# A gated recurrence and a long convolution on one core: batch 0's inputs ahead of the filter, and a filter that is rotated by its loads

## The chip, the cores and the metric

The kernel runs on one core of a Trainium2 chip. The metric is the device time of one execution in microseconds (us), lower is better. The kernel before was run three times: 457.23, 458.74 and 460.05 us, median 458.74. One further execution was recorded by the hardware profiler; all durations below are from it.

## The reference

Inputs are x and f_logit (4 x 6272 x 256), a lower bound per channel, a projection (256 x 768), a filter (6272 x 256) and an output projection (256 x 256), all float32.

```python
sig = 1 / (1 + exp(-f_logit))
f = lower_bound + (1 - lower_bound) * sig
h = f[:, t] * h + (1 - f[:, t]) * x[:, t]      # for t in range(S): a scan over time, per batch and channel
proj = h_all @ w_proj                          # x1, x2, x3: 256 columns each
x2_conv = irfft(rfft(x2, n=S) * rfft(filter, n=S), n=S)   # circular, along time, S = 6272 = 49 * 128
out = (x1 * x2_conv * x3) @ w_out
```

## The kernel before, in words

Time is split as 6272 = 49 x 128, and the Fourier transform is done in two factors by matmuls: one of length 128 (contracted over partitions) and one of length 49 (98 with real and imaginary parts).

For each batch b the work is:

- **hgrn(b)**, L317 to L382: 13 chunks of 512 time steps (the last has 128). Two loads of 512 KB on SyncE's queue (L332), the sigmoid on ScalarE (`sig`, L335), the product with x on GpSimd (`u`, L337), then per half of the channels (`kh`) sixteen transposes on TensorE (`su`, L349), the affine step that makes f (`f`, L362 on ScalarE or L364 on VectorE) and the scan on VectorE (`scan`, L370), which writes h into HA in f16. The start of h is copied behind its end (`wrap`, L378) for the circular shifts.
- **spectrum(b)**, L842: `P` (L714) makes x2 in 13 groups of up to four residues, evacuated by `x2`; it needs all 26 scans of the batch. `F1` (L727) is the transform of length 128, `F2` (L790) of length 49, `prod` the product with the filter's spectrum (on VectorE straight from PSUM, L813, or a copy and a GpSimd product, L822), `I2` (L832) the first inverse factor with its evacuation `Th` (L837).
- **gate(b)**, L385: `x13` (L398) projects x1 and x3, `xs` evacuates x1 and x3 or multiplies them on VectorE (L419), `z` (L428) multiplies on GpSimd. The result lies in `zt`.
- **phase_o(b)**, L882: the second inverse factor `I1` (L895), the gate `y` on VectorE (L901), the output projection `proj` (L913), its evacuation `o` and the store.

Before batch 0 the filter's spectrum is made once, in `prepare` (L436): 13 loads of 512 KB (`ff`, L619: four contiguous rows per partition), a cast to fp32r into `afs` (`fr`, L624), 49 matmuls with a rotated identity `rot` (L630), which put each residue's samples on the right partitions, and two evacuations per group (`f2`, L634) into the two tiles `f2` with gaps between the columns. Then 16 units of `FF1` (L655, two halves each), `afs` (L660), `FF2` (L673) and `hw` (L678), and stores of the spectrum to DRAM (`hst`, L682), from where each unit of each batch loads it again (`H`, L768).

TensorE also has 24 groups `warm` (L600) of four matmuls on the identity, which nothing reads.

The order is written out by hand of a planner: `ORDER` (L124) is a table of words, each an operation's number, the engine that does it and its PSUM bank (`order`, L98). `emit` (L107) issues the operations in the table's sequence, so each engine's queue is in that sequence; the `r` and `w` lists of `op` become semaphore waits by way of the tiles. VectorE's word `MUL` means the direct product (L813, L419). The cost figures in the calls of `op` were the planner's; they issue nothing.

Read out of the table, the order of the kernel before is: the filter's 13 loads first, then the loads of batch 0; on TensorE the 49 rotations with ten `warm` groups among them, then the 16 units of `FF1` and `FF2` interleaved with the transposes of batch 0, then `last`, then `P` of batch 0 (first with `x13` of chunk 0 just before it), then F1, F2, I2 mixed with `x13` of chunks 1 to 12 and the first transposes of batch 1. The other 14 `warm` groups stand later: three in the middle, eleven at the end.

Of the kernel before, what the change touches and what calls it, by code (L numbers as in the profile page):

```python
# [35 lines left out]
WARM = 24  # L36
# [12 lines left out]
AW = 4096  # L49

# [6 lines left out]
def m0_of(r):  # L57
    return (128 * q_of(r) - r) // Q


class Plan:
# [75 lines left out]
    "J0EJ1YGoIGpSJ4FJ3UGqCJ5sJ6YJ7VGvgGwWJ9FGtQGuIGyGG5SG4gHVUHWEJ8WKAQKCAKBRG0uGzYGxYG1YKDBJ+uJ/YG6YG9qG+YHCUG7qHEEH"
    "LWKEYG2QHBgHGsHFYHNGG3AKFTKHDKGWKIuKKUG8YHDYKMEHTQHKgG/SHMYHOYHUAHPuHQYHHYHXUHACKLWHYEKNuKOYHIQHeSHdgHZUHJAHaEHR"
    "WHiqHjYHgqHnQHSGHbUHcMHfYHoYHrAHmgHsYHpoHqYKPTKRDIBWICGHvgHwRKQTHyJKSrH4gHhYHkUHzYHxYH0pH1YHlEIDWILgIEGH5QHtUH7o"
    "H8YH6YHuEIHSIICIFWIGGH9oH+YKTYKUUKWMKVVKZQKXFKYYH2SH3CKbIIUgIJWIMUIKOIOsINYIQEIRYMkQMlAIdgIVSImgIZCMmIH/WIXqIAGI"  # L140
    "YYIWYIPYMoUMpEMqMNEgKaTKcDIvQIwAIaYISWIfYI5gKJYIeSMwQIgKIhYITGIiqIjYIbUMxAMyIKeSIcEKdYNFgKgCM0WM1GInUIzSIrsIsYIp"
    "EIqYNQgIoYJCgI0CIkQIlAM2OKfUKjVKkSKlFKhsNGANHYI6QKmqKnYI8oI+oI/YI9YNRgIxWIyGI1UItSI2EM8WJLgMngIuCI3UI4MI7YJDQJFo"
    "M9GNASJGYNcgJEYJHAJIYM+ONBCJAUKoRKpQNSANTYKqBNCKNIWJBENJGKroKsYKtRKvBJNYNMUJMSNNENKOJOCNOMJUgKuQKyRKzWJPYKwoKxYN"
    "dgJQqNeANogK3XK4SK0BK1GNpgK2YK5HK6qJVUJRYK7YNfYJXENUQNVAK8WNWIK+GNYTNygNzgMrgNZDK9SK/CLAYLBXLCWJJQNaLLGSJZsLDHLE"
    "uLFYNqALIKJKAJaYJSTJTDLHXNgQNkVN8gNhANlFLJvLKYNbgNiILLUNrYLMSLQTLNEJYYLRXLOqNmNLSDLVUKiYLTHN9gLXEM/gJWYNsQNtALWS"
    "NvTLYqLZYN0ANwDLUYLaVLPYNuINxLJbWJcGOHgN1YLbSR8QR9RLfWLcFNnYLdqLeYLgOR+AR/BN+ALkULlMN2SN/YOGgN3CN4KN5QNXYOQgN6AN"
    "7ILhWLiGLmUNDALuSLvKNPYLpWLnELqOOIAOAQOBAOCILjgORgODUObgOagOJYLwSOEELxCLrWLsGLtgOFML4QL5ILogOKSOSANLgLzWONUOlgOk"
    "gL0OOOEOLCL6QL7AL1WL9QL8gL2GOcAMzAOPMOTYOMKL+IMCUOUWOXSOYCMDMVAgOZKU/gL/QOVGOWOMAAOdYMEUMFEMHSMIKOeQOfAOgIOhUVLg"
    "OiEM3YVMgOjMOmASBWSCXSEHSDGMJSMKCOnYOoQOpIOrWOsGOqIMBgNjAOtOVXgLygMMUMRSVYgVNAMNMMSKL3gVBAO2QPAWO8UO3IMLgO9EPBGM"
    "GgPCSPDKPEQPFIO0UO1EVZAO4SO+WOwQO5KO/OVCYOySOzCVaYOuUOvEO6WO7GMOSPGUPHEOxIMPCMWQMXIPMUMQgPKWPLOPNEMTSMUCPIQPOUMY"  # L150
    "WPPEPJIMbQMcISAYPQSPRKPbYMZGPSUPWsPUsP8gPVYPaQPeoPXYSFYPTYPyWPcAPdYPzGMVgSGSSICSHQSLTSJoPqWSNDPiUPmEPuGPYSPZCSMR"
    "SQVSRQQFgPksPnYSOpQOgPlYSSFSToPfYPgSPhCPjYPvYP0UP1ESVXSXHPsuPtYQXgP2QP3IPoSPpCP9UQBsPrYP4WSUYP5GVOYSWQSaRScBP/sQ"
    "qgQAYPwSP6WP7OQHYP+YQCYPxCSbRSdBSYoQGUQIEQJYSeYQKsQzgVDSVECQgQQhAVFKQLYQDWQQYQEGQPUQRsQYQQaAQTsQUYQ8gQkSQlCQMWQc"
    "oQbYRFgQdYQZYSfQQNGSgUQiSQSYShAQjCSkVQmWMagQnGSmNQVQQWAQrSSisSjYVHUVjgQtqQoWQpOQvCQwYSZYVkgSlQSnoSpRQeSVIEVJMQuY"
    "SrBQfCQsYQ0WQ4GQ2uQ3YQ5YRYgVPQVQAVTSVwgVvgRhgQxUVRIVUCVVKQ1YSqXSuWQyESsHStYRQUQ+YSwGRSQRREQ9WQ/uRBuRGSRTARKCQ6UR"
    "HYROQRCYQ7ERIqSoYVGYRPARLYRJYSvWSzTS1DSxuRAYRqgRDUS0XS2vVlAVmYS3YMdQMeAMfgRZSRbqRdqRcYRUWVbQREES4SSPYSyYVKgRVGRW"
    "URXMRaYVcAVxAVdIRMWRjYRNGS5TS7DVfUV7gV8gRrWVnQS6CVyYS8YReYRvGVWYRzgVgMVoAVhMVpIVrSWHgWIgRtGS9XS+UVegVqgS/HTAsVsC"
    "VtKRfVRsYRgFRwYTCXTDQTHRTIWTEHTFoTGYTJBTKuRiURuYRksV9AVzSV0CRmEV3QWSgWRgV1KTMWTLYTOGRnYV+YTNXTPvTRUTTETSVTUtTWWV"
    "4AV5IRxSTQYTXXTbURyCTcVTgSTYGThTTdETZvWJAWKYTetTiKRlYRoQR1YTjrTkYRpAR0UR4ER2sV/WR3YWDQWbgWcgTBYWAGWBOWEATlSTmTTn"
    "CTorTpYTfYR5YTqUTsETrVTttTvSTwUWLWTuYTxCWFITyETzYR6SWMGWNOR7CT0UT1VT2ET3tTVYTaYT5QT6RT7AT8pT9YT+SabQSKYWTAT4YT/K"  # L160
# [34 lines left out]
def kernel(  # L195
# [801 lines left out]
```

## Time and profile before

| what | value |
|---|---|
| median of three runs | 458.74 us |
| span of the profiled execution | 455.6 us |
| TensorE (PE) busy | 439.6 us, 6009 matmuls |
| VectorE (DVE) busy | 407.4 us |
| ScalarE (ACT) busy | 402.3 us |
| GpSimd (POOL) busy | 308.8 us |
| DMA | 120.74 MB, 265 GB/s mean |

The runs shown are of other executions than the profiled one, so the span is not one of the three; it is 3.1 us below their median.

A row of the groups reads: line, engine, operation, output from inputs with their shapes and types, count, then the total busy time and the mean of one in ns, then the idle time before them with what ended it. A row of the stretches reads: start:end, length, busy us of PE, PEld (weight loads), DVE, ACT and POOL with the number of instructions of each, TensorE's granted clock, the DMA share and GB/s. A row of the time line reads: start, length, engine, line, operation. TensorE's matmuls overlap, so the sum over groups is above the busy time of the engine.

### The profile page before, as it was taken

Reading aid. Unit: us, or ns where it says so; the run is one execution under the profiler, and the core shown is the slowest. Engines: PE = TensorE matmul, PEld = TensorE weight load, DVE = VectorE, ACT = ScalarE, POOL = GpSimd, SP = SyncE. Lnnn points to the kernel's source line nnn. Section 1 sums busy time; section 2 is a strip of 40 time slices with the busy share of each in tenths; the row PEclk is TensorE's granted clock in tenths of the full one; section 3 lists DMA queues with packets and bytes.
Section 4 is the critical chain, followed back from the end, with each engine's and each line's share of the span. In section 5 each row is a group of like instructions: output and inputs, shape, how many; then the busy total and the mean of one; then the engine's idle time right before and its main releaser. Section 6 shows DMA issues by size and latency. Waiting matters only on the chain.

```text
span 455.6 us, 14635 instructions
## 1 busy us (share of the span) xinstructions
PE 439.6 (96%) x6009; PEld 348.4 (76%) x6009; DVE 407.4 (89%) x476; ACT 402.3 (88%) x577; POOL 308.8 (68%) x279
## 2 busy tenths in 40 slices
PE   7899999999999999999999999999999999999998
PEld 5687778677767888777668888777778896776797
DVE  8899997799999996999999977999999976989873
ACT  5899999899999987899989998999989858987563
POOL 8888973878899542788995626899994405696400
PEclk9599999999999999999999999999999999999999
DMA  8999999767898985479776896778759721765186
GB/s 326 387 371 345 378 375 361 279 187 233 299 300 282 340 300 237 169 232 374 253 264 219 285 315 272 237 250 303 261 177 317 301 95 46 248 187 185 47 321 246
DMA packets 44434, 120.74 MB, mean 265 GB/s; under 512 B 4304, under 2 KB 7632, under 8 KB 44368
## 3 DMA queue, kind: packets, MB, share of 16 engines
q1 hardware_dynamic: 44368, 119.82, 74.5%
q8 instruction: 47, 0.77, 0.7%
q14 instruction: 19, 0.16, 0.1%
HBM read 86.12 MB, written 31.98 MB: 259 GB/s over the span
## 4 chain that ended last, share of the span: by engine, by line
PE 72%; DVE 11%; ACT 9%; issue 4%; DMA 3%; POOL 1%; SPq 0%; ACTq 0%; DVEq 0%; POOLq 0%
PE PS L398 17%; PE PS L714 9%; PE PS L832 9%; PE PS L913 8%; PE PS L790 7%; DVE HA L370 7%; PE PS L727 6%; PE PS L349 6%; PE PS L895 4%; ACT fTs L362 2%; DMA X<-in_moe_filter_fft_dram 2%; PE PS L600 2%; ACT HA L284 2%; DVE ys L901 1%; ACT X L284 1%
## 5 line engine op out<-in xcount | busy, mean ns | idle before, releaser
L337 POOL TENSOR_TENSOR XT<-XT,FL 128x1024 f32<-128x1024 f32 (+1 forms) x49 | 109.9, 2247 | 55.7 <-ACT FL L335 38.5
L370 DVE TENSOR_TENSOR_SCAN HA<-fTs,HA,PS 128x512 f16<-128x512 f32 (+1 forms) x96 | 112.7, 1202 | 2.0 <-ACT fTs L362 1.1
L398 PE MATMUL PS<-HA,W 128*128 128x490 f16 (+1 forms) x416 | 100.2, 367 | 0.3 <-ACT Th L284 0.2
L822 POOL TENSOR_TENSOR PP<-HA,Hu 98x1008 f16<-98x1008 f16 x42 | 88.0, 2106 | 5.6 <-ACT HA L284 2.6
L284 ACT CAST HA<-PS 128x1024 f16<-128x1024 f32 (+1 forms) x101 | 81.2, 831 | 3.3 <-POOL PP L822 0.8
L901 DVE TENSOR_TENSOR ys<-PS,zt 128x1024 fp32r<-128x1024 f32 (+1 forms) x52 | 58.3, 1151 | 14.0 <-PE PS L895 10.3
L813 DVE TENSOR_TENSOR PP<-PS,Hu 98x1008 f16<-98x1008 f32 x54 | 63.6, 1199 | 1.5 <-PE PS L790 0.7
L362 ACT ACTIVATE fTs<-PS,nomc 128x512 f32<-128x512 f32 (+1 forms) x90 | 59.5, 680 | 4.5 <-PE PS L349 4.2
L398 PEld LDWEIGHTS <-W 128*128 128x128 f16 x416 | 35.3, 97 | 30.2 <-issue 2.9
L428 POOL TENSOR_TENSOR zt<-XS 128x490 f16<-128x490 f32 (+1 forms) x26 | 31.8, 1223 | 39.0 <-DVE ys L901 27.4
L913 PE MATMUL PS<-Wo,ys 128*128 128x256 f32 x392 | 57.5, 293 | 0.4 <-DVE ys L901 0.3
L286 ACT ACTIVATE XS<-PS 128x490 f32<-128x490 f32 (+1 forms) x88 | 51.0, 590 | 6.8 <-DVE zt L419 2.6
L832 PEld LDWEIGHTS <-PP 98*128 98x128 f16 x1024 | 49.2, 98 | 10.1 <-POOL PP L795 1.3
L284 ACT CAST Th<-PS 128x784 f16<-128x784 f32 x63 | 52.0, 828 | 3.4 <-PE PS L832 2.7
L913 PEld LDWEIGHTS PS<-Wo,ys 128*128 128x128 f32 x392 | 49.6, 188 | 4.5 <-DVE ys L901 1.2
L832 PE MATMUL PS<-VA,PP 98*128 98x98 f16 x512 | 52.1, 207 | 0.2 <-POOL PP L795 0.2
L832 PE MATMUL PS<-VB,PP 98*128 98x98 f16 x512 | 51.8, 207 | 0.0
L419 DVE TENSOR_TENSOR zt<-PS,XS 128x490 f16<-128x490 f32 (+1 forms) x78 | 49.2, 648 | 2.7 <-ACT XS L286 0.8
L335 ACT ACTIVATE FL<-FL 128x1024 f32<-128x1024 f32 (+1 forms) x49 | 49.8, 1022 | 0.6 <-DMA FL<-in_f_logit_dram 0.6
L714 PE MATMUL PS<-W,HA 128*128 128x256 f16 x392 | 44.6, 273 | 1.1 <-ACT X L284 1.1
L714 PEld LDWEIGHTS <-HA 128*128 128x128 f16 x392 | 42.9, 142 | 2.0 <-issue 1.3
L349 PE MATMUL PS<-iden,FL 64*128 64x64 f32 x736 | 41.7, 229 | 2.6 <-ACT PP L286 0.6
(119 smaller groups left out, 778.7 us busy)
## 6 DMA issues: line engine op xcount, KB each, us to landing
FL<-in_f_logit_dram SPq DMA_DIRECT2D x45, 512.0 KB, 5.3
XT<-in_x_dram SPq DMA_DIRECT2D x45, 512.0 KB, 6.2
Hu<-H SPq DMA_DIRECT2D x39, 512.0 KB, 4.6
out_dram<-osb SPq DMA_DIRECT2D x24, 512.0 KB, 4.6
out_dram<-PP SPq DMA_DIRECT2D x16, 512.0 KB, 4.8
Hl<-H SPq DMA_DIRECT2D x13, 512.0 KB, 4.7
X<-in_moe_filter_fft_dram SPq DMA_DIRECT2D x9, 512.0 KB, 7.0
out_dram<-HA SPq DMA_DIRECT2D x8, 512.0 KB, 5.7
```

The lines of the kernel that those rows point to most:

```text
L284: nc.scalar.copy(dst, src)
L337: op("u", {"POOL": 0.1 + 0.553 * nb}, lambda e, xt=xt, ft=ft: nc.gpsimd.tensor_tensor(xt, xt, ft, op=AOP.mult), r=[("ft", k)], w=[("xt", k)])
L349: nc.tensor.transpose(bank(pb)[:, at[p] + j:at[p] + hn:nb], src[ps, j, cols], iden[ps, ps])
L362: nc.scalar.activation(fT, sT, AF.Identity, scale=by, bias=1.0)
L370: nc.vector.tensor_tensor_scan(h, fT, bank(pb)[:, 512 - hn:512 + hn], init, op0=AOP.mult, op1=AOP.add),
L398: nc.tensor.matmul(PS[:, p, 0:n], W13[:, kh, js], HA[:, HB[kh] + t0:HB[kh] + t0 + n], start=(kh == 0), stop=(kh == 1))
L714: nc.tensor.matmul(pp[:, r - r0, :], column(HB[kh], q_of(r)), W2[:, kh, :], start=(kh == 0), stop=(kh == 1))
L813: nc.vector.tensor_tensor(pr, px.unsqueeze(1).broadcast_to([TB, 2, UE, 63]), hh(), op=AOP.mult)
L822: nc.gpsimd.tensor_tensor(pr, spec[:, o, :, 1:64].unsqueeze(1).broadcast_to([TB, 2, UE, 63]), hh(), op=AOP.mult)
L832: nc.tensor.matmul(PS[:, ib + o, pr * TB:(pr + 1) * TB], PP[:TB, k, o, n, 2 * pr:2 * pr + 2, :], v[:TB], start=(n == 0), stop=(n == 1))
L901: nc.vector.tensor_tensor(late["ys"][:, yk, :, 0:rn * 128], PS[:, cb:cb + 2, 0:rn * 128], late["zt"][:].rearrange("p k r m -> p k (r m)") ...
L913: nc.tensor.matmul(po[:, i, :], late["ys"][:, yk, kh, i * 128:(i + 1) * 128], Wo[:, kh, :], start=(kh == 0), stop=(kh == 1))
```

## The change

Batch 0 is computed ahead of the filter. Its chunks use six slots instead of four: three in `XF` (x and f together) and three lent by the X2 tile. The filter is loaded behind them. The rotation by matmul is gone: the loads fetch the rows already rotated, as `raw[m] = filter[49 m + 128 q mod 6272]`, group by group of q, each in up to three pieces (below the wrap, above it, and sixteen or more partitions across it from `EF`, a copy in DRAM of the filter's end and start, which two DMAs DRAM to DRAM write). A run of four rows of one partition, 4 KB contiguous before, is four runs of 1 KB now. Each group is then copied straight from the slot into the tiles `f2h` and `f2t` by three copies (`fr`), so one of the two copies per element goes, and the 49 matmuls with it. With `rot` go its two casts on VectorE.

The tiles are placed anew: `zt` is there from the start, so that gate(0) needs no `cz`; `PP`, `Hu`, `zp` and one `osb` are made when `FF1` of units 0 to 6 is done (`turn0`), where `f2h` was. `afs` has three half buffers instead of four halves, so `FF2` is eight matmuls of 256 columns instead of four of 512. `hw` uses the slots of chunk XF[0] for units 0 to 7 (each of its two halves twice), then `Hu` and `osb`. `warm` is eight groups at the start and six among the first transposes. `P` takes its columns in the order of q, and `phase_o` reads them back through `q_of`. `u` may be done on VectorE.

The table is new. Read out of it:

- SyncE: loads of chunks 0 to 4, then 6, 5, 7, 8, 9, 10, with the two `EF` copies between them; the filter's groups 0 to 5 among the loads of chunks 11 and 12; groups 6 and 7 into XF[0], so after the transposes of chunk 12; then 10, 9, 12, 11. 35 loads of filter pieces instead of 13 loads; 22 wraps on this queue instead of 13.
- VectorE: the table arguments (`args0`, `args1`), then for batch 0 24 scans of 512 and two of 128, 17 direct products and 4 evacuations of x1, 3 small table writes and one `f` of 128; then 4 `x2`, 7 `fr` and two gate operations; then, beside `FF1` and `FF2`, 17 `afs`, 5 `hw` and six others; then, up to the first `P` of batch 1, 24 scans of 512 and two of 128, 21 direct products with the spectrum, 11 `y`, 4 `zm` and seven others.
- TensorE: eight `warm`, the 26 transposes (`su`) of batch 0 with 45 `x13` (up to chunk 11) and six `warm` among them, the 13 groups of `P`, then the 16 units of `FF1` and `FF2` with four `F1` and two `x13` among them, `last`, and from there the units of batch 0 with the first seven chunks of batch 1.
- `FF1` of unit 0 needs the first `fr` of all 13 groups.

```diff
-WARM = 24
+WARM = 8
+E0, E1 = 5184, 6272
+NH2 = 56
+def wrap_of(q):
+    return -((128 * q - S) // Q)
...
+    XS = konst.tile([128, 4, XR * Q], F32, name="XS")
+    zt = konst.tile([128, 2, Q, 128], F16, name="zt")
+    EF = dram.tile([2 * (E1 - E0), D], F32, name="EF")
+    lent = X2[:, 0:NX * 4096].bitcast(F32).rearrange("p (k a j d) -> p k a j d", a=2, j=4, d=D)
...
-                k = c % (NX + len(more))
+                k = c % (2 * NX)
...
+                if b == 0 and c < 6 and kh == 0:
+                    op("warm", {"PE": 0.435}, warm, r=["iden"], w=["qT"], take=1)
...
+        slots = [(XF[:, k, a], [(t, k)]) for k in range(NX) for a, t in enumerate(("xt", "ft"))]
+        raws = slots[2:6] + rings + slots[0:2]
+        turns = (0, 1, 2, 3, 4, 5, 6, 7, 0, 1, 2, 3, 6)
+        hws = [(lambda i=i: XF[:, 0, i].rearrange("m r d -> m (r d)").bitcast(F16).rearrange("m (a n) -> m a n", a=2),
+                [("xt", 0), ("ft", 0)][i:i + 1]) for i in range(2)] * 2
...
+        afs = tmp.tile([128, 3, 2, UE // 2, 64], F32R, name="afs")
+        def rows_at(t, n0, m0, m1, q0, rn):
+            o = t[0:1, :]
+            return bass.AP(tensor=o.tensor, offset=o.offset + (n0 + Q * m0 + 128 * q0) * D,
+                           ap=[[Q * D, m1 - m0], [128 * D, rn], [1, D]])
+        for i in range(2):
+            op("ef", {"SP": 0.46}, lambda e, i=i: nc.sync.dma_start(
+                EF[i * (E1 - E0):(i + 1) * (E1 - E0), :].rearrange("(p r) d -> p (r d)", p=64),
+                ff[E0 * (1 - i):E0 * (1 - i) + E1 - E0, :].rearrange("(p r) d -> p (r d)", p=64)),
...
-               lambda e, raw=raw, fr=fr, rn=rn: copy(e, fr[:, 0:rn], raw[:, 0:rn]),
...
-                    nc.tensor.matmul(pr[:, r - r0, :], rot[:, m0_of(r):m0_of(r) + 128],
-                                     fr[:, r - r0, :], start=True, stop=True)
-            for p in range(2):
-                op("f2", either(128 * rn), lambda e, pb, r0=r0, rn=rn, p=p: copy(
-                    e, both(fv[p][:, :, r0:r0 + rn]),
...
+            for i, src, p0, p1, n0 in parts:
+                   nc.sync.dma_start(raw[p0:p1, 0:rn], rows_at(src, n0, p0, p1, q0, rn)),
...
+            for h, (p, j0, nj) in enumerate(((0, 0, NH2), (1, NH2, 64 - NH2), (1, 64, 64))):
+                    copy(e, both(fv[p][:, at:at + nj, q0:q0 + rn]), src[:, j0 // 64, j0 % 64:j0 % 64 + nj])
...
+                for h in range(2):
+                    for r in range(2):
+                        for e2 in range(2):
+                            nc.tensor.matmul(PS[:, pb + e2, 256 * h:256 * h + 256], FTr[rows, r, 0:M],
+                                             afs[rows, at[h], r], start=(r == 0), stop=(r == 1))
...
-                        nc.tensor.matmul(pp[:, r - r0, :], column(HB[kh], q_of(r)), W2[:, kh, :],
+                        nc.tensor.matmul(pp[:, r - r0, :], column(HB[kh], r), W2[:, kh, :],
...
-                        c0 = (rr * Q + r) * 128
+                        c0 = (rr * Q + q_of(r)) * 128
...
+        D1r, FTr = prepare(tmp)
+        hgrn(0)
+        free_x2()
+        last = filters(head, tmp, D1r, FTr)
```

More of the change, by code (lines that the diff above doesn't have):

```diff
@@ L639, in prepare @@
[L639 to L646 removed]
+            op("warm", {"PE": 0.435}, warm, r=["iden"], w=["qT"], take=1)
@@ L840, in unit, with spectrum @@
            r=["cv"], w=[("Th", u)], src=i2)
-    def spectrum(b):
+    def spectrum(b, last=None, turn=None):
         phase_p(b)
@@ L847, in spectrum @@
                 phase_f1(b, u)
+            if last and q == 0:
+                small_spectrum(last, turn)
             mini(b, q)
```

389 lines of the change are left out of this document (192 added, 197 removed).

## The prediction

> **What bounds the kernel now.** I read the page first (busy shares, slices), then the busy time by stretches, then the time line at the borders of the stretches.
>
> ```profile
> PE 439.6 (96%) x6009; PEld 348.4 (76%) x6009; DVE 407.4 (89%) x476; ACT 402.3 (88%) x577; POOL 308.8 (68%) x279
> ```
>
> TensorE (PE) is busy for 96%, so it looks like the bound. But three engines lie close together, and the stretches show that they take turns:
>
> ```profile
> core 0: us, PE busy (x) PEld busy (x) DVE busy (x) ACT busy (x) POOL busy (x), PEclk, DMA share, GB/s
> 0.00:23.00 23.00, 18.40 (x90) 14.37 (x91) 19.13 (x49) 15.76 (x25) 19.75 (x40) 0.78 0.93 358
> 23.00:71.50 48.50, 45.74 (x598) 36.34 (x599) 46.99 (x53) 48.29 (x74) 40.64 (x44) 1.00 1.00 367
> 71.50:97.00 25.50, 24.96 (x262) 20.16 (x261) 19.85 (x22) 22.96 (x31) 17.32 (x14) 1.00 0.78 270
> 97.00:143.10 46.10, 45.49 (x696) 32.12 (x693) 44.82 (x52) 45.03 (x69) 40.17 (x32) 1.00 0.84 272
> 143.10:167.10 24.00, 23.35 (x422) 20.48 (x421) 23.83 (x25) 23.10 (x34) 13.37 (x10) 1.00 0.88 308
> 167.10:455.60 288.50, 281.65 (x3952) 224.90 (x3950) 252.76 (x281) 247.17 (x348) 177.52 (x142) 1.00 0.67 235
> ```
>
> Up to 23 us only the filter is rotated. From 23 to 71.5 ScalarE (48.29 of 48.5) and VectorE (46.99) are the bound: the scans of batch 0 run beside the filter's FF1 and FF2. At 71.5 FF2 is done and P of batch 0 starts; from 97 on all three engines are full, VectorE with 68.65 of 70.1 us (98%). At 167.1 P of batch 1 starts, and it can't start before batch 1's last scan:
>
> ```profile
> 163.65 2.37 DVE HA L370 x2
> 166.06 1.08 PE PS L895 x32
> 167.14 10.65 PE PS L714 x96
> ```
>
> So the border to watch is P of batch 1. What TensorE has left from there is the same in both tables but for three groups of warm, so I carry the 288.5 us over and work out when the border falls.
>
> **The change, part by part.** What goes on TensorE:
>
> ```profile
> L630 PE MATMUL PS<-afs,rot 128*128 128x256 f32 x49 | 11.7, 388 | 2.5 <-POOL afs L296 2.4
> L600 PE MATMUL PS<-iden 128*128 128x256 f16 x96 | 14.0, 307 | 1.4 <-POOL iden masks.py:199 1.4
> 447.45 1.48 PE L600 MATMUL PS<-iden 128*128 128x256 f16 x12
> ```
>
> The rotations (11.7 us) and ten warm groups lie before 23 us, where TensorE has nothing else: alone they bring nothing. Three warm groups in the middle (twelve matmuls, 1.48 us by the last row) lie where it is full: -1.5 us. Eleven stand at the end behind or between the last waits: 0. What the new order can win is the useful work in the first 23 us; what it can lose is overlap. I add it up along the engine that ends each stretch last.
>
> *1. Start of the scans.* They queue on VectorE behind the table arguments, whose last operations are these, first with GpSimd busy beside them, then with it mostly idle, and GpSimd's u:
>
> ```profile
> 4.68 1.27 DVE L517 TENSOR_SCALAR PP<-HA 128x520 f32<-128x520 f32 x1
> 5.99 1.28 DVE L518 TENSOR_SCALAR PP<-PP 128x520 f32<-128x520 f32 x1
> 7.31 1.44 DVE L519 TENSOR_TENSOR PP<-HA,PP 128x520 f32<-128x520 f32 x1
> 12.44 0.42 DVE L517 TENSOR_SCALAR PP<-HA 128x512 f32<-128x512 f32 x1
> 12.89 0.43 DVE L518 TENSOR_SCALAR PP<-PP 128x512 f32<-128x512 f32 x1
> 13.35 0.69 DVE L519 TENSOR_TENSOR PP<-HA,PP 128x512 f32<-128x512 f32 x1
> L337 POOL TENSOR_TENSOR XT<-XT,FL 128x1024 f32<-128x1024 f32 x45 | 107.0, 2381 | 48.3 <-ACT FL L335 31.3 <-DMA XT<-in_x_dram 11.8 <-PE PS L913 3.2
> ```
>
> They end at 14.0. After the change GpSimd runs the products u of chunks 0 to 2 just then (2.4 each), so the second three may cost up to 3.99 instead of 1.54: 14.0 to 16.5, I take 15.5. The two casts of rot (0.6 us) go, but the arguments wait for the index tables all the same: 0. [...]
>
> *2. Batch 0's scans with its gate.* On VectorE, and x13 (the row without a line is of all of L349 on TensorE):
>
> ```profile
> L370 DVE TENSOR_TENSOR_SCAN HA<-fTs,HA,PS 128x512 f16<-128x512 f32 x88 | 109.2, 1268 | 1.6 <-ACT fTs L362 1.1
> L370 DVE TENSOR_TENSOR_SCAN HA<-fTs,HA,PS 128x128 f16<-128x128 f32 x8 | 3.6, 474 | 0.3
> L419 DVE TENSOR_TENSOR zt<-PS,XS 128x490 f16<-128x490 f32 x71 | 45.5, 658 | 2.6 <-ACT XS L286 0.8 <-PE PS L398 0.5 <-issue 0.2
> L398 PE MATMUL PS<-HA,W 128*128 128x490 f16 (+1 forms) x416 | 100.2, 367 | 0.3 <-ACT Th L284 0.2
> 0.00:455.60 455.60, 66.41 (x1568) 0.99 0.75 265
> ```
>
> 24 x 1.268 + 2 x 0.474 + 21 x 0.658 + 1.9 small = 47.1. Means overlap the next start: the same kind of sum for 71.5 to 167.1 gives 95.9 where the stretches show 88.5 busy, so x 0.92: 43.4, and 1.1 for waits. Nothing else binds here: 26 of 104 su (66.4) and 45 of 208 x13 (100.2) take TensorE 38 us; ScalarE has lost the f2 copies; the loads are 12.8 MB of inputs, 1 of weights, 2.2 of EF and 3 of the first filter groups, 19 MB, at 367 GB/s 52 us. The last scan ends at 15.5 + 44.5 = 60.0.
>
> *3. P, and the filter's tail.*
>
> ```profile
> 71.51 8.07 PE L714 MATMUL PS<-W,HA 128*128 128x256 f16 x72
> X<-in_moe_filter_fft_dram SPq DMA_DIRECT2D x9, 512.0 KB, 7.0
> FL<-in_f_logit_dram SPq DMA_DIRECT2D x45, 512.0 KB, 5.3
> H<-Hu SPq DMA_DIRECT2D x4, 512.0 KB, 7.1
> ```
>
> 98 matmuls at 8.07/72 = 11.0: P ends at 71.0. FF1 also needs all 13 filter groups. Groups 6 and 7 wait for XF[0], free after the transposes of chunk 12, about 2.5 us before the last scan (57.5). Group 12 waits behind fr of group 6, and group 11 behind it on SyncE: 5.3 to 7.0 to land, about 2 for three fr, 5.3 to 7.0 again, 0.6 for the copy: 70.7 to 74.1. I take 72.5 for FF1. Of the 39 fr 21 are on GpSimd; they and P's evacuations lie beside P. The 35 issues at about 0.4 us and nine more wraps on SyncE lie beside the scans, but for the sixteen of groups 6 to 12, which are in the tail.
>
> *4. FF1 and FF2, now by themselves.*
>
> ```profile
> 22.82 2.94 PE L655 MATMUL PS<-D1r,f 128*128 128x256 f32 x20 [0.77 <-ACT f L284]
> 25.69 1.35 PE L673 MATMUL PS<-afs,FTr 64*128 64x512 f32 x8
> L673 PE MATMUL PS<-afs,FTr 64*128 64x512 f32 x64 | 10.8, 436 | 0.2 <-ACT afs L284 0.2
> L727 PE MATMUL PS<-D,X 128*128 128x128 f16 x512 | 36.3, 219 | 1.5 <-ACT X L284 1.4
> L289 DVE CAST afs<-PS 128x512 fp32r<-128x512 f32 x12 | 7.8, 676 | 1.0 <-PE PS L655 0.6 <-PE PS L673 0.4
> ```
>
> 128 x 0.147 = 18.8; 64 x 0.169 = 10.8; four F1 of 64 (36.3) 2.3, two x13 0.96, one F2 about 0.5: 33.4 of TensorE. Halving FF2's matmuls is not in the trace. If the row halves overlap as now (64 x 436 ns fit into 10.8 us), a unit is four pairs at 0.147 instead of 0.68 (-1 us over 16 units); if not at all, eight at 0.147 (+8): I take +1, near the overlapped end. The ring of two hw slots makes units 4 and 6 wait for stores of units 1 and 3: three units later is 6 us, the store lands 7.1 after its issue: 0 to 3, I take +1. Sum 35.4: unit 15 is done at 107.9. VectorE has 17 afs, 5 hw (1.2) and six others here, about 22 us; **13 us of it lie idle** which the kernel before filled with scans.
>
> *5. Batch 0's spectrum to P of batch 1*, on VectorE:
>
> ```profile
> L813 DVE TENSOR_TENSOR PP<-PS,Hu 98x1008 f16<-98x1008 f32 x54 | 63.6, 1199 | 1.5 <-PE PS L790 0.7
> L901 DVE TENSOR_TENSOR ys<-PS,zt 128x1024 fp32r<-128x1024 f32 x48 | 56.8, 1212 | 11.2 <-PE PS L895 7.5 <-PE PS L913 3.3
> L749 DVE TENSOR_TENSOR zp<-PS,X 98x128 f16<-98x128 f32 x32 | 10.7, 372 | 1.0 <-PE PS L743 0.8
> ```
>
> 24 x 1.268 + 2 x 0.474 + 21 x 1.199 + 11 x 1.212 + 4 x 0.372 + 5.4 for seven others = 76.7, x 0.92 = 70.6, at the 98% of 97 to 167.1 72.0. TensorE's work here is about 61 us, so it no longer binds. P of batch 1: 107.9 + 72.0 = 179.9, where it was 167.1. The x13 that TensorE did early don't help: they were work for an engine that waits here.
>
> *6. Sum.* 179.9 + 288.5 - 1.5 = 466.9 of span, and 3.1 between the profiled span (455.6) and the median (458.74): **470.0 us**, 2.5% slower. The bounds: all low ends together (14.0; no waits in 2; FF1 at P's end; FF2 -1 and no ring) give 14.0 + 43.4 + 11.0 + 32.4 + 72.0 + 287.0 + 3.1 = 462.9; the high ends of 1, 3, 4 (16.5, +1.6, +7, +2) add 11.6: 482.
>
> **The rivals.**
>
> *Faster.* TensorE stays the only bound, and useful work starts when the first products are there: x lands near 7 (the second load, 5.3 to land by the row of FL), u takes 2.4, so at 9.5 instead of 22.8. Then the end comes 13.3 earlier, 1.0 is given back to FF2 and 1.5 of warm comes on top: 458.7 - 13.8 = 445. For it: PE at 96%, and ScalarE, the bound from 23 to 71.5, loses some ten copies of 0.6 us. Against it: VectorE's 98% from 97 on. It decides from the point where the 13 us of step 4 are refilled or the stretch of step 5 takes VectorE 58 us. 15%.
>
> *No change.* The low ends hold together: 462.9, or a little less. 14%.
>
> *Slower still by the clock.* The clock fell while TensorE was thinly used:
>
> ```profile
> 10.00:12.00 2.00, 1.31 (x8) 0.78 (x7) 1.90 (x7) 2.00 (x5) 1.77 (x2) 0.82 1.03 412
> 12.00:20.00 8.00, 7.45 (x30) 6.04 (x31) 6.16 (x14) 5.93 (x11) 6.05 (x11) 0.50 1.00 376
> ```
>
> It was 1.00 in 23 to 71.5 with 94% busy. Step 2 needs about 41 us of 51 with the six warm, 80%, between the two. At half clock 38 us are up to 76, the last scan 25 us late; if it holds for a third of the stretch, 478. 6%. [...]
>
> *The loads don't rotate for free.* Runs of 1 KB move at half the rate: the last 3.3 MB take 18 us instead of 9, FF1 at 81: 479. Nothing of this size with 1 KB runs is in the trace. 6%.
>
> **How the numbers follow.** My case has 59%, by itself 464 to 477. A measurement of this kernel can tell about 1% (454.2 to 463.3) from no change. Faster 15%, same 14% (the low ends), slower 59 + 6 + 6 = 71%. The range runs from 457 to 482: it leaves out the faster case and the upper ends of the two slow ones.
>
> **What would show it.** Right: P of batch 0 near 60, FF1 near 72 and FF2's end near 107, VectorE under 65% busy between these two; VectorE at 97% or more from there to P of batch 1 near 179; no L630 line; a rest of about 287. Wrong: a last scan well before 57; VectorE with idle time in step 5; a clock under 0.9 after 25 us; FF1 waiting on a filter load after 75; a rest that differs from 287 by over 4 us, which the steps can't see.

## The result, and the profile after

The changed kernel takes 489.93 us (median of 4 runs, 488.47 to 496.15), the kernel before 458.25 us beside it: the ratio is 1.0684, 95% interval 1.064 to 1.0728. The forecast was 470.0 us with a range to 482. The longest of the four runs, 496.15 us, lies over 1.5% above the fastest, counts as a slow run and is left out of the ratio. The direction is right; the loss is 31 us where 11 were forecast.

Busy times of the page, the first line that the prediction showed of before:

```profile
PE 439.5 (90%) x5984; PEld 343.1 (70%) x5984; DVE 416.9 (86%) x475; ACT 398.1 (82%) x563; POOL 313.0 (64%) x300
```

TensorE is busy as long as before (439.6), so the whole 31.1 us of span (486.7 against 455.6) are idle time of TensorE. The busy time by stretches, cut at the borders of the prediction's steps, tells where:

```profile
core 0: us, PE busy (x) PEld busy (x) DVE busy (x) ACT busy (x) POOL busy (x), PEclk, DMA share, GB/s
0.00:14.00 14.00, 9.74 (x84) 7.27 (x84) 12.09 (x32) 5.45 (x6) 11.22 (x24) 0.84 0.82 302
14.00:59.60 45.60, 40.19 (x462) 22.86 (x459) 43.16 (x53) 42.05 (x69) 36.93 (x32) 0.97 1.01 331
59.60:81.70 22.10, 13.13 (x99) 11.47 (x97) 11.40 (x13) 12.97 (x18) 17.29 (x21) 0.85 0.95 198
81.70:114.80 33.10, 32.52 (x308) 27.44 (x309) 22.91 (x30) 25.77 (x35) 12.59 (x39) 1.00 0.76 253
114.80:191.60 76.80, 65.67 (x1145) 55.04 (x1144) 70.99 (x71) 65.30 (x90) 54.74 (x45) 0.96 0.84 288
191.60:486.70 295.10, 278.30 (x3898) 218.99 (x3894) 256.40 (x280) 246.53 (x349) 180.24 (x143) 0.99 0.68 237
```

TensorE is idle for 4.3 + 5.4 + 9.0 + 0.6 + 11.1 + 16.8 = 47.2 us; before it was 16.0, of them 6.9 from P of batch 1 on. The borders against the forecast:

| border | forecast | after | forecast length | length after |
|---|---|---|---|---|
| P of batch 0 | 60.0 | 59.63 | 60.0 | 59.6 |
| FF1 | 72.5 | 81.79 | 12.5 | 22.2 |
| unit 15 of FF2 done | 107.9 | 114.8 | 35.4 | 33.0 |
| P of batch 1 | 179.9 | 191.63 | 72.0 | 76.8 |
| end of the span | 466.9 | 486.7 | 287.0 | 295.1 |

So four terms are off: +9.7, -2.4, +4.8 and +8.1 (and -0.4 for the first), together 19.8 us. The first of them on TensorE's time line (start, length, instruction, and in brackets the idle time before it and what ended it):

```profile
58.70 0.84 DVE L376 TENSOR_TENSOR_SCAN HA<-fTs,HA,PS 128x128 f16<-128x128 f32 x2
```
```profile
59.63 2.13 PE L746 MATMUL PS<-W,HA 128*128 128x256 f16 x17
63.60 1.18 PE L746 MATMUL PS<-W,HA 128*128 128x256 f16 x9 [1.84 <-DMA HA<-HA]
65.40 5.40 PE L746 MATMUL PS<-W,HA 128*128 128x256 f16 x48 [0.63 <-DVE X L293]
72.30 1.03 PE L746 MATMUL PS<-W,HA 128*128 128x256 f16 x8 [1.49 <-DVE X L293]
78.31 3.35 PE L746 MATMUL PS<-W,HA 128*128 128x256 f16 x16 [4.98 <-ACT X L288]
81.79 1.68 PE L664 MATMUL PS<-D1r,f2h 128*128 128x256 f32 x12
```

The last scan (VectorE, first fence) ends when the forecast said. Then P, 11 us of work, takes 22. Its first wait, 1.84 us, is for a wrap (HA<-HA), which goes through the same DMA queue (SPq) as the filter's pieces. Its longest is the last: the last group waits for a copy of P on ScalarE, and that copy stands in ScalarE's queue behind a copy of a filter piece that hasn't landed:

```profile
77.05 0.30 ACT L288 CAST f2t<-XF 128x64 fp32r<-128x64 f32 x1 [7.73 <-DMA XF<-in_moe_filter_fft_dram]
77.26 1.01 ACT L288 CAST X<-PS 128x1024 f16<-128x1024 f32 x1
```

The filter's pieces come at 198 GB/s though the DMA engines are busy for 95% (row of 59.60); in 14 to 59.6, with the inputs of batch 0, it was 331 at a share of 1.01.

### The profile page after: what moved, and what is told of

The parts are those of the page before. It is cut to its first block, busy times and chain, and to the rows that moved or that the text cites. A ratio compares the mean times of both kernels' runs of the same rounds, so it can differ in the third digit from the quotient of the medians.

```text
span 486.7 us, 14615 instructions
## 1 busy us (share of the span) xinstructions
PE 439.5 (90%) x5984; PEld 343.1 (70%) x5984; DVE 416.9 (86%) x475; ACT 398.1 (82%) x563; POOL 313.0 (64%) x300
## 4 chain that ended last, share of the span: by engine, by line
PE 40%; DVE 22%; DMA 18%; issue 7%; ACT 6%; POOL 3%; SPq 3%; DVEq 0%; ACTq 0%; POOLq 0%
PE PS L404 10%; DVE HA L376 7%; PE PS L866 6%; PE PS L949 5%; PE PS L822 5%; DMA XF<-in_moe_filter_fft_dram 4%; PE PS L759 3%; PE PS L353 3%; DMA XF<-in_x_dram 3%; DVE ys L937 3%; DMA Hu<-H 3%; DVE PP L847 3%; DMA out_dram<-HA 2%; DMA XF<-in_f_logit_dram 2%; PE PS L746 2%
## 5 line engine op out<-in xcount | busy, mean ns | idle before, releaser
L341 POOL TENSOR_TENSOR XF<-XF 128x1024 f32<-128x1024 f32 (+1 forms) x42 | 93.1, 2220 | 63.5 <-DMA XF<-in_x_dram 42.0
L856 POOL TENSOR_TENSOR PP<-HA,Hu 98x1008 f16<-98x1008 f16 x43 | 90.2, 2106 | 5.2 <-ACT HA L288 2.7
L368 ACT ACTIVATE fTs<-PS,nomc 128x512 f32<-128x512 f32 (+1 forms) x94 | 61.9, 674 | 8.8 <-PE PS L353 5.7
L847 DVE TENSOR_TENSOR PP<-PS,Hu 98x1008 f16<-98x1008 f32 x53 | 62.1, 1199 | 7.4 <-DMA Hu<-H 6.3
L353 PE MATMUL PS<-iden,XF 64*128 64x64 f32 x1376 | 60.6, 232 | 7.1 <-POOL XF L341 2.9
L353 PEld LDWEIGHTS PS<-iden,XF 64*128 64x128 f32 x1376 | 51.9, 144 | 19.5 <-issue 4.5
L404 PEld LDWEIGHTS <-W 128*128 128x128 f16 x416 | 35.6, 97 | 39.0 <-issue 11.2
L338 ACT ACTIVATE XF<-XF 128x1024 f32<-128x1024 f32 (+1 forms) x46 | 46.4, 1008 | 13.4 <-DMA XF<-in_f_logit_dram 13.4
L746 PE MATMUL PS<-W,HA 128*128 128x256 f16 x392 | 46.0, 278 | 9.5 <-ACT X L288 5.5
L434 POOL TENSOR_TENSOR zt<-XS 128x490 f16<-128x490 f32 (+1 forms) x30 | 37.0, 1239 | 23.5 <-DVE ys L937 18.1
L288 ACT CAST Th<-PS 128x784 f16<-128x784 f32 x56 | 45.8, 822 | 5.6 <-PE PS L866 4.5
```

The costliest lines, as they stand in the source:

```text
L288: nc.scalar.copy(dst, src)
L341: nc.vector if e == "DVE" else nc.gpsimd).tensor_tensor(
L353: nc.tensor.transpose(bank(pb)[:, at[p] + j:at[p] + hn:nb], src[ps, j, cols], iden[ps, ps])
L368: nc.scalar.activation(fT, sT, AF.Identity, scale=by, bias=1.0)
L404: nc.tensor.matmul(PS[:, p, 0:n], W13[:, kh, js], HA[:, HB[kh] + t0:HB[kh] + t0 + n], start=(kh == 0), stop=(kh == 1))
L746: nc.tensor.matmul(pp[:, r - r0, :], column(HB[kh], r), W2[:, kh, :], start=(kh == 0), stop=(kh == 1))
```

## The experiments

Ratios are to the kernel before, timed beside each on the same chip; the changed kernel's own is 1.0684 [1.064, 1.0728].

**1. Why the filter's pieces are slow.** Three suspects first, each removed in the changed kernel: the runs of 1 KB (e1), the copies of the wrap rows in DRAM and their readers (e2), the strided order in which the copies read (e3), and all three together (e4).

```
e1, e4  nc.sync.dma_start(raw[p0:p1, 0:rn], rows_at(...))
        -  ap=[[Q * D, m1 - m0], [128 * D, rn], [1, D]]
        +  ap=[[Q * D, m1 - m0], [1, rn * D]]            # 4 KB runs, other rows
e2, e4  -  op("ef", ..., nc.sync.dma_start(EF[...], ff[...]))
        +  op("ef", ..., None);  pieces of part 2 read ff instead of EF
e3, e4  -  src = raw[:, 0:rn].rearrange("m r (p e g) -> m p g e r", p=2, e=2)
        +  src = raw[:, 0:rn] flat, the first 2 * nj * rn elements   # other elements
```

> The changed kernel, but each piece of the filter reads four contiguous rows per partition (runs of 4 KB) instead of four runs of 1 KB; same number of DMAs, bytes and waits. The filter's rows are then the wrong ones. Theory A (the short runs halve the DMA rate, and the filter's tail ends late because of it): the stretch of the filter's loads (46 to 80 us in the changed kernel, 200 to 225 GB/s) moves above 330 GB/s, FF1 starts near 73 instead of 82, and the time falls by 7 to 10 us, to 480 to 483. Rival B (the pieces are late because of the chain of slots, copies and issues on SyncE, not of the rate): FF1 stays after 79 and the time within 3 us of 490. Rival C (the loss is the order, VectorE idle beside FF1 and FF2): time may fall with FF1, but at least 20 us above the kernel before stay.

> The changed kernel without the two copies DRAM to DRAM; the pieces across the wrap read rows of the filter itself (wrong ones), in the same runs of 1 KB. If these 2.2 MB, copied beside the loads of chunks 5 to 10, delay the scans or the filter: 2 to 5 us less. If they lie beside VectorE's work as predicted: within 1.5 us of the changed kernel, 488 to 491.

> The changed kernel with the copies fr reading contiguous elements of the slot instead of elements 1 KB apart (so the filter's order is wrong); same sizes and same output pattern. In the changed kernel a copy of 448 takes 0.92 to 1.02 us on each engine where 0.57 was expected. If the stride of the reads is what costs: 448 falls to about 0.6 us. If these copies hold up the filter's tail (theory: copies, not loads): time falls 5 us or more. If the loads do (theory A): time falls by 0 to 3 us, and FF1 stays after 79.

> Long runs, no DRAM to DRAM copies and contiguous reads in the copies, all three at once. If the filter's way into the tiles is the whole loss against my sum, FF1 starts near 72.5 and the time comes to 470 to 480, and what stays above the kernel before (458) is the order of the work: VectorE with 10 us or more idle beside FF1 and FF2, and P of batch 1 near 180 instead of 167. If the order costs nothing: 460 or less.

Measured: 491.0 us (1.0747 [1.0693, 1.0801]), 493.66 (1.0822 [1.0767, 1.0877]), 492.52 (1.0775 [1.072, 1.083]) and 491.96 (1.0752 [1.0706, 1.0798]). None gains in the total. With 4 KB runs (e1) the rate is 194 GB/s in 60 to 70 us and 213 in 70 to 80; FF1 comes at 82.1 to 84.8 in the four. So none of the three is what holds FF1 back by itself, the 1 KB runs of the prediction's rival among them.

Two smaller things can be read here. The strided reads do make the copies long, as e3 supposed: a copy of 448 elements takes 1.01 us on ScalarE in the changed kernel and 0.64 in e3, without FF1 coming earlier for it (first the changed kernel, then e3):

```profile
L288 ACT CAST f2h<-HA 128x448 fp32r<-128x448 f32 x2 | 2.0, 1006 | 0.0
```
```profile
L288 ACT CAST f2h<-HA 128x448 fp32r<-128x448 f32 x2 | 1.3, 636 | 0.0
```

And from P's start to FF1 e1, e2 and e3 take 22.6, 22.7 and 23.9 us (22.2 in the changed kernel), but e4 18.9: together the three may be worth some 3 us there, by one trace.

The same question put to the kernel before, whose loads cover all partitions:

```
 nc.sync.dma_start(raw[:, 0:rn],
-    ff[:, r0:r0 + rn, :])
+    ff[:, r0 // 4:r0 // 4 + 12 * (rn - 1) + 1:12, :])    # 1 KB runs, other rows
```

> The kernel before, with its 13 whole filter loads (128 partitions) read as runs of 1 KB from rows 12 apart instead of 4 KB at a stretch (other rows of the filter go into the transform). Theory that 1 KB runs move at half the rate: the 6.4 MB take about 16 us more at the start, FF1 later by that, and the time rises by 10 to 16 us. Theory that run length does not matter (4 KB runs in the changed kernel gained nothing): within 2 us of before.

460.29 us, 1.005 [1.0021, 1.0079]: 2.3 us, where half the rate, which the expectation only assumed, would cost over 10. From 8 to 16 us the DMA engines moved 348 GB/s in e5 and 412 in the kernel before. Left are the partitions that a load covers (16 to 112), the distance of its rows in DRAM, and the number of loads:

```
e6  one load a group, all partitions:   - raw[p0:p1, 0:rn] (2 or 3 of them)   + raw[0:128, 0:rn]
e15 34 loads (after: 35), all partitions, one or two rows each:               + raw[0:128, c0:c1]
    (both: rows 12 apart in a partition, other rows; the wrap copies are not read)
e7  pieces as after, neighbouring rows: - [[Q * D, m1 - m0], [128 * D, rn], [1, D]]
                                        + [[rn * D, m1 - m0], [D, rn], [1, D]]
```

> The changed kernel, with one load of all 128 partitions for each of the 13 filter groups, in 1 KB runs (rows 49 apart from partition to partition, 12 apart in a partition; other rows of the filter), in place of two or three pieces of 16 to 112 partitions; the copies of the wrap rows stay but are not read. Theory that loads on few partitions are slow: the rate between 50 and 80 us rises from 200-250 to over 300 GB/s, the last group of P follows the others without a wait, FF1 starts at 72 to 75 instead of 81.7 and the time falls by 7 to 10 us. Theory that it is the distance of the rows in DRAM, or the order in which copies and loads wait for one another: FF1 stays at 80 or later, the time within 3 us of the changed kernel.

> The changed kernel with its pieces of 16 to 112 partitions, read from neighbouring rows in DRAM (4 KB from partition to partition instead of 49 KB; other rows of the filter). Theory that the distance of the rows makes the pieces slow: rate over 300 GB/s between 50 and 80 us, FF1 at 72 to 75, the time 7 to 10 us below the changed kernel. Theory that loads on few partitions are slow: 200 to 250 GB/s as before, FF1 at 80 or later, within 3 us of the changed kernel.

> The changed kernel with as many filter loads as it has (35, two or three a group), each of all 128 partitions and of one or two of the group's four rows, in place of 16 to 112 partitions and four rows. Theory that few partitions make a load slow: the same as with one whole load a group, over 300 GB/s per full busy share between 50 and 80 us, FF1 at 75 to 78, the time within 2 us of that run (486.8). Rival, that it is the number of loads: 200 to 250 GB/s, FF1 at 80 or later, the time that of the changed kernel.

The row of 60 to 70 us, in order of the changed kernel, e7, e6 and e15 (the last two numbers are the DMA engines' busy share and GB/s):

```profile
60.00:70.00 10.00, 7.54 (x68) 7.12 (x66) 4.12 (x6) 8.47 (x12) 7.27 (x10) 1.00 0.97 201
```
```profile
60.00:70.00 10.00, 7.44 (x62) 6.46 (x60) 4.79 (x8) 8.34 (x14) 7.96 (x11) 1.00 1.01 212
```
```profile
60.00:70.00 10.00, 9.15 (x82) 8.87 (x81) 7.22 (x7) 7.98 (x12) 10.00 (x13) 1.00 0.69 226
```
```profile
60.00:70.00 10.00, 9.37 (x80) 8.64 (x79) 8.69 (x10) 9.21 (x14) 10.00 (x13) 1.00 0.88 258
```

Divided by the share, as an estimate for engines that are busy throughout, that is 207, 210, 328 and 293 GB/s: near rows change nothing, full partitions do, and with nearly as many loads as before they do so almost as well. Issue to landing shows it too: three pieces of 320 KB took 9.0 us (median) in the changed kernel, whole loads of 512 KB 6.2 in e6:

```profile
XF<-in_moe_filter_fft_dram SPq DMA_DIRECT2D x3, 320.0 KB, 9.0
```
```profile
XF<-in_moe_filter_fft_dram SPq DMA_DIRECT2D x10, 512.0 KB, 6.2
```

From P's start to FF1 it takes 22.2 us after, 21.7 in e7, 16.7 in e6 and 17.8 in e15. The last group of P and FF1 in e6:

```profile
73.00 3.57 PE L748 MATMUL PS<-W,HA 128*128 128x256 f16 x16 [3.21 <-ACT X L288]
76.55 2.72 PE L666 MATMUL PS<-D1r,f2h 128*128 128x256 f32 x12
```

So the partitions are the cause of 4 to 5.5 of the 9.7 us. Of the rest the trace of e6 shows 3.2 us of P's last group behind the same copy on ScalarE; that was not tried apart. FF1 came at 76.55 in e6 and 78.89 in e15, later than the 72 to 75 and 75 to 78 that were expected. In the total little is left of it, where 7 to 10 us were expected of e6: e6 took 486.78 us (1.0632 [1.0566, 1.0698]), e15 487.27 (1.0657 [1.0608, 1.0706]), e7 493.54 (1.072 [1.0643, 1.0797]). The intervals overlap with that of the changed kernel. The next stretches took back most of the lead: e6 is 5.2 us ahead at FF1, 3.8 at the end of FF2 and 1.7 at P of batch 1.

**2. What sets P of batch 1.** VectorE's waits from 114.8 to 191.6 us (total, times, longest):

```profile
DVE PP L847 <- DMA Hu<-H: 4.7, 3, 2.4
DVE HA L376 <- ACT fTs L368: 1.1, 2, 0.9
```

The spectrum of the filter is loaded late, behind its own stores. e8 lets every such load read the first pair of units (another unit's spectrum, the same bytes); e16 takes e6 and leaves out most of each output tile of batch 0, so that little is stored beside the loads of batch 1:

```
e8   - turned(H[u // 2][u % 2])        + turned(H[0][u % 2])
e16  - nc.sync.dma_start(to, of)       + nc.sync.dma_start(to[:, 0:1], of[:, 0:1])   # batch 0
```

> The changed kernel, whose loads of the filter's spectrum (L800) all read the first pair of units, so that they wait for the first store and not for the latest (the products use the wrong units' spectrum; amount and shape of the loads are the same). Theory that late spectrum loads hold VectorE up between FF2's end and P of batch 1: the three waits of VectorE on a spectrum load (4.7 us) and 6.9 us of SyncE's waits on stores go, P of batch 1 comes 3 to 6 us earlier and the time falls by as much. Rival, that the loads wait for their slots, for bandwidth and for SyncE's queue, not for the store: within 2 us of the changed kernel.

> The changed kernel with one whole load for each filter group, and with only a quarter (of one slot a half) of each output tile of batch 0 stored (the rest of that output is left out, some 5 MB of 6.4). With whole loads alone FF2 ended 3.9 us earlier, the scans of batch 1 ran 5.6 us earlier up to 174, and P of batch 1 came only 1.7 us earlier: inputs that landed late beside the output stores, at a full DMA share between 160 and 180 us. Theory that this meeting of loads and stores holds P of batch 1 up: P of batch 1 at 182 to 187 instead of 190.0, the time 2 to 6 us below that run (486.8). Rival, that the order of the operations holds it: within 2 us of that run.

e8: 492.03 us (1.0733 [1.0672, 1.0795]), no gain. The wait on the spectrum shrinks to 2.5 us, but the stretch takes 80.0. e16: 484.59 us (1.0582 [1.053, 1.0634]), 2.2 below e6; P of batch 1 at 189.27, 0.7 earlier, and the stretch took 77.9. Neither theory holds: e8 gains nothing, and e16 lies 2.2 us lower, at the edge of what was expected, but not by way of P of batch 1, which was expected at 182 to 187. In all of them VectorE works 71 to 72 us there and idles for 6 to 8, mostly in waits of 0.2 to 2.5 us on other engines: take one away and others fill its place.

**3. The part from P of batch 1 on.** At that border the same work is left in both kernels but for warms and a handful of operations, so the tails of the two tables can be exchanged: all operations up to P of batch 1 stay, the others follow in the order, and on the engines and PSUM banks, of the other table. Where a bank was still in use at the seam, another was taken.

```
 ORDER = [entries of its own table up to "P, batch 1, group 0"]
-        + [the rest of its own table]
+        + [the same operations in the order, engines and banks of the other table]
```

> The kernel before up to P of batch 1; from there the same work (all but two operations on the same engines) in the order, engines and banks of the changed kernel's table, 45 banks renumbered where they were taken. Theory that the new table is the worse one from there on (295.1 us after, 288.5 before): the time rises by 5 to 9 us, the part from P of batch 1 takes 293 to 297. Rival, that the rest is longer because of what the changed kernel leaves behind (late loads, stores of the spectrum, clock): within 2 us of before.

> The changed kernel up to P of batch 1; from there the order, engines and banks of the table of before, 21 banks renumbered. Theory that the new table is the worse one: the part from P of batch 1 takes 286 to 290 us instead of 295.1 and the time falls by 5 to 9 us, to 481 to 485. Rival, that it is what the changed kernel leaves behind: within 2 us of the changed kernel.

> The kernel before up to P of batch 1, then the order, engines and banks of the changed kernel's table, as in the run with the new tail, but with 2 banks renumbered instead of 45. Theory that the new table is by itself the worse one from P of batch 1 on: 462 to 467 us (the rest takes 293 to 297 instead of 288.5), and the 30 us of the first graft came from its renumbered banks. Rival, that the new tail suits the state at P of batch 1 as well as the old: within 2 us of before. If it is near 490 again, a tail doesn't fit another head at all, and the graft says nothing of the new table.

> The changed kernel up to P of batch 1, then the order, engines and banks of the table of before, none renumbered (the first such graft had 21). Theory that the new table is the worse one: the rest takes 286 to 290 us instead of 295.1, the time 481 to 485. Rival, that the rest is longer because of what the changed kernel leaves behind at P of batch 1: within 2 us of the changed kernel, or above it.

| kernel | head | tail | banks renumbered | tail takes | time | ratio |
|---|---|---|---|---|---|---|
| before | old | old | 0 | 288.5 | 458.25 | 1 |
| e13 | old | new | 2 | 303.3 | 472.82 | 1.0328 [1.0286, 1.037] |
| e10 | old | new | 45 | 319.8 | 489.94 | 1.0726 [1.0652, 1.08] |
| after | new | new | 0 | 295.1 | 489.93 | 1.0684 [1.064, 1.0728] |
| e14 | new | old | 0 | 289.1 | 487.71 | 1.0661 [1.06, 1.0722] |
| e11 | new | old | 21 | 304.9 | 503.02 | 1.0991 [1.0924, 1.1058] |

The rows of e14 and of e13 from P of batch 1 on:

```profile
199.70:488.80 289.10, 275.54 (x3896) 219.27 (x3894) 249.19 (x277) 250.12 (x352) 177.67 (x142) 0.99 0.68 238
```
```profile
169.58:472.90 303.32, 286.23 (x3953) 225.26 (x3950) 256.27 (x281) 244.81 (x346) 184.26 (x145) 0.99 0.65 226
```

With the old tail the changed kernel needs 289.1 us from P of batch 1 on; with its own it needs 295.1, and the new tail took 292.9 to 296.6 us in the eleven other traces with the changed kernel's table (e1 to e4, e6 to e9, e15 to e17), whether P of batch 1 came at 189.3 or at 198.4. The old tail on the old head took 287.2 to 290.8 in four traces (before, e5, e12, e18). So about 6 of the 8.1 us that the forecast missed belong to the new table, not to what the change leaves behind. The other 2 are within what the old tail varies by, and the 1.5 us that the sum credited for the warm groups don't show.

By the total this is not shown. e14's 487.71 us missed the expected 481 to 485: it is 2.2 us below the changed kernel, inside the intervals. In its profiled execution P of batch 1 came at 199.67, with the same code up to there and later than in any of those twelve traces (see the last section).

e13 missed its expectation as well (303.3 us for the tail where 293 to 297, 472.82 in all where 462 to 467 were expected). Its tail isn't quite the same work: it keeps the 14 warm groups of the kernel before, which the new table has no place for, and seven of them lie in the middle of P of batch 1:

```profile
179.65 3.22 PE L597 MATMUL PS<-iden 128*128 128x256 f16 x28 [1.10 <-ACT X L281]
```

So e13 fits the new tail being the slower one, but gives no price for it. The first pair of grafts missed its expectation by some 20 us and told nothing of the tables. It told something else: e10 has the order and engines of e13 but other bank numbers in 96 entries of its table, e11 those of e14 but for seven places and other bank numbers in 45 entries, of some 1,480 in the tail, and each took 15 to 17 us more.

**4. FF1 and FF2 by themselves.** Two pairs. In the first, three of four matmuls of FF1 are left out (most of the spectrum is not computed); in the second, VectorE does twelve of its copies twice.

```
e9, e12   - for i in range(4): nc.tensor.matmul(pa[:, i, :], ...)    + for i in range(1): ...
e17, e18    copy(e, af, ...)         # on VectorE, twelve times:
          + nc.vector.tensor_copy(src, src)
```

> The changed kernel with one of the four matmuls in each half of FF1 (the other three are left out, so most of the spectrum is not computed): 96 matmuls of about 0.147 us, 14.1 us of TensorE less in the 33.1 us of FF1 and FF2. Theory that FF1 and FF2 now stand by themselves on the path: FF2 ends 7 to 12 us earlier (the copies, 25.8 us on ScalarE, bind next) and the time falls by 6 to 12 us. Rival, that the loss lies in the loads and in the table behind it: below 3 us.

> The kernel before with the same 96 matmuls of FF1 left out. Theory that FF1 and FF2 are covered there by the scans of batch 0, with ScalarE (48.3 of 48.5 us) and VectorE (47.0) as the bound: the time falls by 0 to 4 us. Rival, that TensorE alone bounds the kernel before: it falls by 10 to 14 us.

> The changed kernel, in which VectorE does twelve of its copies after FF1 twice (the second writes the PSUM bank onto itself): 12 x 0.69 = 8.3 us more of VectorE in the 33.1 us of FF1 and FF2, where it was busy for 22.9. Theory that VectorE lies idle there and that this idle time is what the change pays with: the time rises by 0 to 3 us. Rival, that the order of its instructions leaves no room there either: 5 us or more.

> The kernel before with the same: twelve copies of VectorE after FF1 twice, 12 x 0.68 = 8.1 us more between 23 and 71.5 us, where VectorE was busy for 47.0 of 48.5. Theory that scans fill VectorE beside FF1 and FF2 there: the time rises by 5 to 9 us. Rival, that ScalarE alone binds that stretch and VectorE has room: 0 to 3 us.

e12, the kernel before: 459.66 us, 1.0037 [1.001, 1.0064]; the time doesn't fall, as expected. But the 14.1 us were not taken out cleanly: the granted clock in that stretch is 0.83 where it was 1.00, and TensorE is busy from FF1's start to the end of FF2 for 43.2 us where it was 45.5. The row of e12 from 21.5 to 73 us:

```profile
21.50:73.00 51.50, 43.61 (x503) 30.94 (x503) 47.93 (x53) 48.85 (x76) 41.48 (x46) 0.83 1.00 359
```

TensorE is idle for 7.9 us of it (2.8 of 48.5 before) and the stretch is no shorter, which speaks for ScalarE and VectorE as its bound. e9, the changed kernel: 492.53 us (1.0781 [1.0687, 1.0875]), against the expectation; FF2 still ends at 115. The row of its second half shows TensorE as busy as ever, at a granted clock of 0.57:

```profile
100.00:115.00 15.00, 14.70 (x103) 11.16 (x101) 10.33 (x15) 9.89 (x13) 6.24 (x15) 0.57 0.97 318
```

The work that is left takes longer at that clock: eight matmuls of FF2 last 1.22 us there and 0.74 in the changed kernel at 1.00. So the run can't tell whether TensorE is on the path.

e18: 465.53 us, 1.0156 [1.012, 1.0192], 7.1 of the 8.1 us added, as expected: VectorE has hardly any room beside FF1 and FF2 in the kernel before. e17: 495.22 us, 1.0816 [1.0774, 1.0859], 6.0 us above the changed kernel's ratio, where 0 to 3 were expected. The total alone would not show it, since e2, with no work added, came to 1.0822. The stretch does: FF1 to the end of FF2 took 37.6 us, and 33.0 to 35.6 in the thirteen other traces of the changed kernel and its variants. TensorE's waits there that end with a second copy (L695 is FF2, L671 FF1, L629 the second copy):

```profile
PE PS L695 <- DVE PS L629: 2.4, 3, 1.3
PE PS L671 <- DVE PS L629: 1.2, 3, 0.5
```

So 8.3 us of such copies don't fit into VectorE's 10.2 idle us: TensorE waits 3.6 us for them. They also hold a PSUM bank longer, and the run can't tell whether work that holds none would fit.

## Why the prediction was wrong, point by point

- *Step 1 and 2, start and end of batch 0's scans*: right, the start in part by luck. The first scan starts at 14.04 (forecast 15.5), the last ends at 59.5 (60.0). Beside two of GpSimd's u (8.14 to 13.12 us) two of the arguments' operations took 2.32 and 2.47 us, where the kernel before had 0.42 and 0.43, so the three took 5.5 us where the forecast allowed 3.99 at most. They also began at 8.58 instead of 12.44, which the forecast didn't work out, and the two misses cancel:

```profile
8.58 2.32 DVE L518 TENSOR_SCALAR X<-HA 128x512 f32<-128x512 f32 x1
10.93 2.47 DVE L519 TENSOR_SCALAR X<-X 128x512 f32<-128x512 f32 x1
13.44 0.69 DVE L520 TENSOR_TENSOR X<-HA,X 128x512 f32<-128x512 f32 x1
14.04 2.32 DVE L376 TENSOR_TENSOR_SCAN HA<-fTs,PS 128x512 f16<-128x512 f32 x2
```

- *Step 3, "P ends at 71.0 ... I take 72.5 for FF1"*: the step that failed most, +9.7 us. It took the landing of a piece (5.3 to 7.0) from loads of 128 partitions, 0.6 us for a copy, and let the copies "lie beside P". The pieces cover 16 to 112 partitions and move at about 207 GB/s at a full share, where loads of 128 partitions move at 293 to 328 (e6, e7, e15): that is 4 to 5.5 us. The copies on ScalarE take 0.98 to 1.1 us instead of 0.6, because they read with a stride (e3), and they share ScalarE's queue with P's own copies, so that P itself waits for the filter. What makes a load of fewer partitions slower, the runs don't show. The prediction looked only for run length.
- *Step 4, 35.4 us*: 33.0; FF2 as eight matmuls takes 0.71 to 0.75 us a unit, the split costs the +1 that was taken, and the ring of hw slots cost nothing that can be seen. That VectorE idles there is right in size (10.2 us, 13 forecast); whether this time could be used otherwise stays open (e17).
- *Step 5, "at the 98% of 97 to 167.1 72.0"*: VectorE's work was right (70.99 us busy, 70.6 forecast), its share was not: 92%. The 98% did not carry over to the new order. Which wait makes the difference can't be settled: it isn't the spectrum's loads (e8) nor the output stores (e16) alone.
- *Step 6, "I carry the 288.5 us over"*: wrong by 8.1 us. In the trace of e14 about 6 of them go with the new order of the same work; in the total they are not shown.
- *The rivals.* Faster and no change: out. "The loads don't rotate for free" had FF1 at 81 and 479 us: the place and the delay are right, its cause (1 KB runs) is not (e1, e5). Half the rate was the author's assumption, which no run shows: with runs of 1 KB on all partitions the kernel before lost 2.3 us (e5). Half clock in step 2: not in the profiled execution (0.97), but in other executions of the same head it falls in part (to 0.84 in e14, last section).

The errors of steps 3, 5 and 6 have one sign: the sum took each stretch at the efficiency that the old table had there. Why the new table reaches less is argued only: a written-out order keeps its waits short where pieces and copies take the time that it was made for, and here they take longer.

## What to carry to other kernels

Cost a load by the partitions that it covers, not by its bytes alone: splitting a load of 128 partitions into pieces for a free rotation cost about a third of its rate here (207 GB/s at a full share against 293 to 328). A share of busy time (98%) and the length of an untouched tail belong to the order in which they were measured; when a change brings a new table, neither can be carried over. Exchanging tails at a border can price a table by itself, if the work left is really equal and the bank numbers stay: of four grafts here one did. Before an idle engine's time is called free, see whether what it waits for waits for it: 8.3 us of copies put into 10.2 idle us made the stretch 4.6 us longer here.

## What the runs showed of the hardware that was not expected

The changed kernel's first stretch varies, and the granted clock with it. Up to P of batch 0, e8, e9, e11, e14 and e17 run the code of the changed kernel, yet P came at 58.98, 57.93, 62.16, 62.98 and 63.24 us, at mean clocks from 14 to 60 us of 0.96, 1.00, 0.91, 0.84 and 0.90, and at 59.63 and 0.97 after. The rows of e9 and e14:

```profile
14.00:60.00 46.00, 40.69 (x471) 23.81 (x469) 44.35 (x54) 43.02 (x73) 39.05 (x34) 1.00 1.03 335
```
```profile
14.00:60.00 46.00, 40.20 (x435) 22.89 (x435) 41.91 (x47) 38.87 (x63) 34.02 (x29) 0.84 0.91 313
```

At a mean clock of 1.00 P starts at 57.93, at 0.84 at 62.98: TensorE is busy for as long in both, with 36 matmuls less in the second. Whether the clock fell first or TensorE had to wait first, the runs don't tell. The totals spread as well: the four runs of e9 from 489.64 to 495.93 us, those of e14 from 484.32 to 490.59, twelve runs of the kernel before beside e9 from 456.1 to 460.26.

Work taken off TensorE did not come back as time: with 14.1 us of its matmuls left out, the granted clock between FF1 and the end of FF2 was 0.83 in e12 and 0.74 in e9 (1.00 in both kernels with them), and TensorE's busy time there fell by only 2.3 and 2.7 us.
